# Linear attention and MLP on one core: splitting the second pair's columns from loaded columns, not storing and reloading the split, and one load moved in SyncE's queue

## The chip, the cores and the metric

The kernel runs on one core of a Trainium2 chip. The metric is the device time of one execution in microseconds, median of three runs. A core has five engines with queues of their own: TensorE (PE in the profile; its weight loads are PEld), VectorE (DVE), ScalarE (ACT), GpSimd (POOL) and SyncE (SP). In this kernel nearly all transfers are issued from SP's queue, in the order of the program; the bias additions come from POOL's.

## The reference, cut to what matters

Input x is 2048 rows (S) of 512 columns (D); F is 1376; there are 32 heads of 16 columns.

```python
def _A_ref(x, wqkv, wo):                  # linear attention
    q, k, v = ...x @ wqkv...              # 32 heads
    phi = lambda t: jnp.where(t > 0, t + 1, jnp.exp(t)) + 1e-6
    pq, pk = phi(q), phi(k)
    kv = jnp.einsum("bhsd,bhse->bhde", pk, v)
    z = jnp.einsum("bhsd->bhd", pk)
    num = jnp.einsum("bhqd,bhde->bhqe", pq, kv)
    den = jnp.einsum("bhqd,bhd->bhq", pq, z)[..., None] + 1e-6
    return (num / den) @ wo               # heads side by side
def _B_ref(x, w1, b1, w2, b2):            # MLP, squared relu
    r = relu(x @ w1 + b1)
    return (r * r) @ w2 + b2
xn = _layernorm(x)
return x + _A_ref(xn, wqkv, wo) + _B_ref(xn, w1, b1, w2, b2)
```

## The kernel before, in words

**Tiles and blocks.** The 2048 tokens are 16 tiles of 128 rows, and four tiles make a block of 512 tokens (blocks 0 to 3). Each float32 operand of a matmul is used as two parts, a rounded high part (`h`) and the rest (`l`), and a product takes three matmuls (high by high, high by low, low by high; `three`, L127). ACT makes a high part by a copy; DVE makes the low part by a subtraction (`split` L117, `rest_of` L121).

**First half of the program (to about 100 us): keys and the key-value sums.** For each tile in turn SP loads rows of x, the row statistics are taken and the tile is normalised (L248), turned into columns (`transposed`, L312) and split into `xs..h` and `xs..l` (tiles of `xsb`, two pairs: `xsb[0]` = xs0, `xsb[1]` = xs1; blocks 0 and 2 use xs1, blocks 1 and 3 use xs0). Matmuls project the keys (`pk`, L369) and sum keys times tokens (`kx`, L389). Tiles 0 to 3 are turned by PE. From tile 4 on the turning goes by way of HBM: `regroup` (L277) stores the normalised tile (`via`, L281), then four loads bring it back regrouped (`xg`, issued by `move`, L289), and DVE transposes 32 by 32 blocks (`turn`, L293). Columns of tiles 0 to 7 (blocks 0 and 1) are stored unsplit in HBM as well (`xTd`, L336). Those of blocks 2 and 3 stay on chip (`xT2`, `xT3`). The row tiles x0/x1, x2/x3, x12/x13 and x14/x15 share two buffers in turn (`two`, L91): the load of tiles 14 and 15 takes the buffer of tiles 2 and 3. It stands behind `normalise(*single)`, which normalises tile 4 and issues its store, in the program and so in SP's queue (L656, L657).

**Stored parts.** In this half, at tiles 4 and 7, the split columns of blocks 0 and 1 are stored to HBM too, high and low part each as one transfer of 1 MB (`xsd`, L807 to L811), since their buffers are needed again for blocks 2 and 3.

**Second half: two phases `n`.** Phase 0 (to about 252 us) computes the outputs of blocks 3 and 2 (`t1`, `t2`), phase 1 those of blocks 1 and 0. In each phase queries and the MLP's first layer are formed for the pair of blocks by seven-product block multiplications (`product`, L484). Their operands are the split columns `x1`, `x2` (xs0, xs1), sums of column halves (`T`, made from unsplit columns by `sums_of`, L751) and split weight chunks (`aop`, made by `operands_first`, L771, in the buffers of the unsplit columns xT2 and xT3). The remainder of w1 that fills no chunk of 128 is multiplied on its own by `plain_1` (L478), from a split chunk `z` (`w1z`). The second layer and the attention output accumulate in four PSUM banks (`acc`) and are added to the residual rows (`res`, L1054) and stored.

**End of phase 0, where most of the change lies (L1248 to L1341).** PE sums the second layer of block 2 over the hidden tiles in the order of `waiting`, then attention (`add_attention`), then the last two hidden tiles (`last_two`: hidden tile 0 and the remainder, number 10). Their parts are made by `wait_for` (L1225): ACT squares and copies, DVE subtracts. In the steps `e` of the loop the next phase is prepared: the unsplit columns `f1`, `f2` of blocks 1 and 0 come back from `xTd` into xT3 and xT2 (L1254), the four stored parts are reloaded into xs0 and xs1 (L1300 to L1302, one for each of `e` = 1 to 4), the remainder of w1 is loaded at `e` = 4 (`small_chunk`, L785; DMAs of L184) and split at `e` = 7, and two chunks of wqkv are loaded at `e` = 5 (L714).

**What sets the order.** The order on every engine and queue is written out by hand (`manual_schedule`, L76): an engine takes its instructions as the program emits them. The lists `AT` and `AE` and the tuple at L1303 place small steps.

Of the kernel before, what the change touches and what calls it, by code (L numbers as in the profile page):

```python
# [18 lines left out]
def kernel(  # L19
# [71 lines left out]
    def two(name):  # L91
        return keep.tile([P, 2, 512], F32, name=name, tag=next_tag("x"))
# [7 lines left out]
    def f32(ap):  # L100
        return ap.bitcast(F32)
# [7 lines left out]
    def copy(eng, o, i, bias=0.0):  # L109
        if eng == "act":  # L110
            nc.scalar.activation(o, i, AF.Copy, bias=bias)  # L111
        elif bias:
            ENG[eng].tensor_scalar(o, i, bias, None, op0=OP.add)
        else:
            ENG[eng].tensor_copy(o, i)

    def split(h, l, src, eh, el):  # L117
        copy(eh, h, src)
        ENG[el].tensor_tensor(out=l, in0=src, in1=f32(h), op=OP.subtract)  # L119

    def rest_of(l, src, h):  # L121
        nc.vector.tensor_tensor(out=l, in0=src, in1=f32(h), op=OP.subtract)  # L122
# [21 lines left out]
        pair(f"pair_{k}")  # L144
    dram = ctx.enter_context(tc.tile_pool(name="dram", bufs=1, space=bass.MemoryType.DRAM))
    xTd = [dram.tile([P, NJ, BT], F32, name=f"xTd{b}") for b in range(NB // 2)]
    xsd = [[dram.tile([P, NJ, BT], F32, name=f"xsd{b}{u}") for u in "hl"] for b in range(NB // 2)]
    w2s, wos = {}, {}
    ident = keep.tile([P, P], F32, name="ident", tag="ident")
    heads = work.tile([P, P], F32, name="heads", tag="heads")  # L150
# [6 lines left out]
    def load_x(i, t):  # L157
        n = t.shape[1]
        nc.sync.dma_start(t, xf[i * P:(i + n) * P, :].rearrange("(i p) d -> p i d", i=n))
        for k in range(n):  # L160
            xr[i + k] = t[:, k]
# [18 lines left out]
    def raw_1(f):  # L180
        t = w512(f"r1_{f}", "raw", 6)
        tj = t.rearrange("p (j n) -> p j n", j=NJ)
        for a, o, n in units(f):
            nc.sync.dma_start(tj[:, :, a:a + n], w1[:, o:o + n].rearrange("(j p) n -> p j n", j=NJ))  # L184
        return t
# [62 lines left out]
    def normalise(tiles, st, mv, y):  # L248

        n = len(tiles)  # L250
        r, u = (y[:, k, :n] for k in range(2))
        if tiles[-1] >= NPE:

            nc.vector.scalar_tensor_tensor(u, mv[:, :n, 0], -1.0, r, op0=OP.mult, op1=OP.mult)
        later = []

        def last(i, o, src, k):
            nc.scalar.activation(o, src, AF.Identity, bias=u[:, k:k + 1], scale=r[:, k:k + 1])
            if i in groups:
                regroup(i)  # L260

        for k, i in enumerate(tiles):
            o, src = xp[i], xr[i]
            if i >= NDVE:

                o, src = o.rearrange("p g (j c) -> p g j c", j=NJ), gjc(src)
            if i < NPE:
                nc.vector.tensor_scalar(o, src, mv[:, k, 0:1], r[:, k:k + 1], op0=OP.subtract, op1=OP.mult)
                if i in groups:
                    regroup(i)  # L270
            else:
                later.append(lambda a=(i, o, src, k): last(*a))
        return later
# [25 lines left out]
    def cols(i):  # L299

        return xsb[(i // TB + 1) % 2]
# [77 lines left out]
    def phi_k(i, ps, mid=lambda: None, late=lambda: None):  # L379
        kp[i] = w512(f"k{i}", "p", 6)  # L380
        phi(ps, kp[i], mid, late)
# [265 lines left out]
    single = group(4)  # L647
    soon = group(5)
    normalise(*fourth)
    phi_k(0, pks[0])  # L650
    measure(single)
    tokens(0)
# [1 line left out]
    parts(0)  # L654
    phi_k(1, pks[1])
    normalise(*single)  # L656
    load_x(14, two("x14"))  # L657
    parts(1)
    tokens(1, "dve")
    measure(soon)  # L660
# [57 lines left out]
    def load_1(kind, n):  # L718
        load = raw_1 if kind == "w" else raw_q
        return [load(2 * n + k).rearrange("p (c n) -> p c n", c=2) for k in range(2)]  # L720
# [50 lines left out]
    def operands_first(n, w):  # L771

        o = {}

        def first():
            aop.update({k: keep.tile([P, 2, 2, 512], F32R, name=f"aop{n}_{k}", tag=f"xT{NB // 2 + k}") for k in range(2)})
            chunk_split(0, 0, w[0])

        def sums():
            o[0], o[1] = chunk_sums(0, w)  # L780

        return [first, sums, lambda: chunk_split(0, 1, o[0]), lambda: last_split(0, w[1][:, 1]),
                lambda: chunk_split(1, 0, o[1])]

    def small_chunk(z):  # L785
        t = raw_1(NF - 1)
        return lambda: split(z[:, 0], z[:, 1], t, "act", "dve")

    extra, counts = [], [[0, 0, 0, 0, 0, 1, 1, 0, 0, 1, 2, 2, 0, 1, 4, 1, 2]]

# [10 lines left out]
    for i in range(2, NT):  # L801
        if i == 13:
            nc.sync.dma_start(b1s[:, :NF - 1], b1[:(NF - 1) * P].rearrange("(f p) -> p f", p=P))
            for a, o, n in units(NF - 1):
                nc.sync.dma_start(b1s[a:a + n, NF - 1:], b1[o:o + n, None])
        move()
        if i in (4, 7):  # L807

            b = i // 7
            for u in range(2):  # L810
                nc.sync.dma_start(xsd[b][u], f32(cols(b * TB)[u]))  # L811
        if i == 9:
            load_o()
        if i > 10:
            fetch()
        ps = pks[i] if i < 3 else bank(f"pk{i}")
        if i > 2:
            project(i, ps, wk, HL)
        high = low = keep_t = lambda: None
        if i < NDVE:  # L820
            high, low, keep_t = transposed(i + 1)
        later = normalise(*soon) if i == 3 else []

        soon_turned = transposed(i + 2) if 11 <= i and i + 2 < NT else ()

        def mid():
            high()
            more(i)

        def late():  # L830
            low()
            more(i)

        if i == 12:
            rawz = raw_1(NF - 1)
            T.update({n: tokens_sum(n, f"B{n - 1}") for n in (1, 2)})
        if i == 12:
            w = load_1("q", 0)
        if i == 13:
            todo_1 = operands_first(0, w)  # L840
            extra.append(todo_1.pop(1))
        if i == 14:
            z = pair("w1z0")
            extra.append(lambda: split(z[:, 0], z[:, 1], rawz, "act", "dve"))
            o34 = halves(four("Tf", "r0"))
            extra.extend(sums_of(xT[NB - 1], xT[NB - 2], *o34))
            lows = [extra.pop() for k in range(2)]
            extra += [todo_1[0], lows[1], todo_1[1], lows[0], *todo_1[2:]]
        phi_k(i, ps, mid, late)
        more(i)  # L850
        run(*soon_turned)
        if i != 3:
            later = normalise(*soon) if soon else []
        parts(i)
        keep_t()
        if i == 2:
            tokens(2)
        if i + 1 < NT:
            tokens(i + 1)
        run(*later)  # L860
        if NDVE < i + 2 < 13:
            run(*transposed(i + 2))
        pieces(int(i > 11))
        if i == 2:
            ahead[3] = statistics(6, 7)
        if i + 2 in (4, 6, 8, 10):
            ahead[i + 2] = group(i + 6, i + 7)
        if i < 10:
            measure(ahead[(i + 2) // 2 * 2], i % 2)
        soon = ahead.get(i + 1, ())  # L870
        if soon:
            roots(*soon)
        kx(i - 1)
        more(i)
# [66 lines left out]
    for n in range(2):  # L941
# [343 lines left out]
        for e, f in enumerate(waiting[:-2]):  # L1285
            mlp_2(acc, f, s.pop(f))
            if e + 3 < NF - 2:
                wait_for(waiting[e + 3])
            if e:
                do(w2next, 2)  # L1290
                if e + 8 < NF:
                    g = waiting[e + 8]
                    w2next.extend(piece_2(g, place(g)))
            if e == 2:
                load_res(t2)
            if e == 4:
                bias = add_bias()
            if e in ((5, 6) if n else (7, 8)):
                do(bias)
            if n == 0 and 1 <= e < 5:  # L1300
                k, u = divmod(e - 1, 2)
                nc.sync.dma_start(f32((x1, x2)[k][u]), xsd[(t1, t2)[k] - 2][u])  # L1302
            do(prepare, (1, 0, 0, 1, 0, 2, 2, 3, 1, 3, 1)[e])  # L1303
            if n == 0:
                if e == 4:
                    z = pair("w1z1")
                    zs = small_chunk(z)
                if e == 5:
                    w = load_1("q", 0)
                if e == 7:  # L1310
                    zs()
            step(AE[e])
            if e and 0 < len(parts_2) and len(steps[t2]) <= 5 * (len(parts_2) - 1):
                do(parts_2)
# [2 lines left out]
        do(parts_2, NJ)  # L1317
        for k in range(TB):
            add_attention(acc, t2 * TB + k, n == 1 and k == last)
            if k < 2:  # L1320
                wait_for(last_two[1 - k])
            if n == 0:
                if k == 0:
                    prepare = operands_first(1, w)
                if k in (0, 2):
                    do(prepare, 2 if k == 0 else 3)
# [43 lines left out]
```

## Time and profile before

| | |
|---|---|
| median of three runs | 410.08 us (409.76 to 411.25) |
| profiled execution | 410.41 us |
| its span, first to last instruction | 408.7 us |
| PE / DVE / ACT busy | 403.8 / 304.7 / 262.2 us |
| bytes moved by DMA | 56.87 MB |
| granted PE clock | 0.999 |

A row of the chain of work that ended last gives start, length and what ran or was waited for. "SPq" and "DVEq" are a queue's own time for an issue, "DMA a<-b" a transfer that was waited for. A row of the timeline gives start and length, the engine, the line, the operation, out<-in, shapes and a count; in brackets the idle time ahead of it and what ended it. For an SP row the length is the time of the issue, not of the transfer. A row of groups ends with the count, the busy time and the mean in ns, then the idle time ahead and its cause. A row of stretches gives the stretch, its length, and busy time and count for each engine, then PE's clock, the mean busy share of the DMA engines and GB/s. A row of waits gives total, times and longest.

### The profile page before, as it was taken

The page shows a single profiled execution, that of the slowest core. Times are in us where ns is not written, and L with a number is a line of the kernel's source. Part 1 is how long each engine was busy: PE and PEld are TensorE (multiplying, and loading weights), DVE is VectorE, ACT ScalarE, POOL GpSimd, SP SyncE. Part 2 cuts the span into 40 slices and gives each one's busy share as a digit, 9 for nine tenths or more (in the row PEclk, how much of TensorE's full clock was granted, in tenths as well). Part 3 has the DMA queues.
Part 4 walks back from the last instruction along what each step waited for, and adds up shares of the span by engine and source line. Part 5 has one row for each costly group of instructions (what it writes and reads, how often), then busy time and mean ns, then how long its engine had stood idle before and what let it go on. Part 6 is the DMA issues. An engine that isn't in the chain of part 4 may idle for free.

```text
span 408.7 us, 5630 instructions
## 1 busy us (share of the span) xinstructions
PE 403.8 (99%) x1943; PEld 331.7 (81%) x1943; DVE 304.7 (75%) x556; ACT 262.2 (64%) x459; POOL 48.5 (12%) x81
## 2 busy tenths in 40 slices
PE   8999999999999999999999999999999999999996
PEld 7878888888788888888878887888888888878885
DVE  6886667487898989988349956567989586449833
ACT  4656777556888788886818641677587857837520
POOL 6343333220000000030000300000000200001200
PEclk9999999999999999999999999999999999999999
DMA  6969576810432231381557983321121881024612
GB/s 213 332 210 329 204 309 206 254 31 0 119 91 79 77 103 28 109 204 22 215 204 271 326 194 106 113 53 51 51 79 36 229 189 36 2 103 154 105 26 103
DMA packets 47182, 56.87 MB, mean 139 GB/s; under 512 B 8305, under 2 KB 30577, under 8 KB 45874
## 3 DMA queue, kind: packets, MB, share of 16 engines
q1 hardware_dynamic: 44850, 52.32, 39.3%
q0 software_dynamic: 2304, 4.20, 6.3%
q8 instruction: 15, 0.25, 0.2%
q14 instruction: 13, 0.11, 0.1%
HBM read 41.69 MB, written 13.63 MB: 135 GB/s over the span
## 4 chain that ended last, share of the span: by engine, by line
PE 85%; DMA 6%; DVE 5%; issue 1%; SPq 1%; ACT 1%; POOL 1%; DVEq 0%; ACTq 0%
PE b L488 33%; PE acc L130 29%; PE pk L369 9%; PE kx L389 9%; DMA r<-in_B_w_dram 4%; PE acc L499 2%; PE pz L130 1%; DVE s L119 1%; SPq L289 1%; PE b L130 1%; PE pz0b L130 1%; DMA x<-in_A_x_dram 1%; DMA via<-xp 1%; DMA xg4s<-via 1%; PE pt L308 0%
## 5 line engine op out<-in xcount | busy, mean ns | idle before, releaser
L130 PE MATMUL acc<-w2r,s 128*128 128x512 f32 x477 | 113.1, 390 | 0.4 <-DVE s L119 0.4
L130 PEld LDWEIGHTS acc<-w2r,s 128*128 128x128 f32 x477 | 89.4, 188 | 20.1 <-DVE s L119 0.8
L488 PE MATMUL b<-T,aop 128*128 128x512 f32 x336 | 83.4, 389 | 0.0
L488 PEld LDWEIGHTS b<-T,aop 128*128 128x128 f32 x336 | 63.0, 188 | 13.9 <-ACT t L111 0.8
L1046 POOL DMA_DIRECT2D res<-in_B_b_dram x16 | 14.4, 1091 | 277.2 <-DVE dt L430 87.4
L389 PE MATMUL kx<-pk,tok 128*128 128x512 f32 x192 | 46.3, 390 | 0.0
L389 PEld LDWEIGHTS kx<-pk,tok 128*128 128x128 f32 x192 | 35.9, 188 | 7.6
L488 PE MATMUL b<-xs0h,aop 128*128 128x512 f32 x112 | 36.9, 390 | 0.0
L130 PE MATMUL acc<-mh,aTsr 128*128 128x512 f32 x112 | 35.6, 389 | 0.0
L1054 DVE TENSOR_TENSOR res<-acc,res 128x512 f32<-128x512 f32 x16 | 11.0, 692 | 21.5 <-PE acc L130 19.2
L488 PEld LDWEIGHTS b<-xs0h,aop 128*128 128x128 f32 x112 | 21.0, 188 | 4.4
L130 PEld LDWEIGHTS acc<-mh,aTsr 128*128 128x128 f32 x112 | 21.0, 188 | 4.4
L119 POOL TENSOR_TENSOR tok<-xp,tok 128x512 fp32r<-128x512 f32 x15 | 19.8, 1322 | 38.9 <-ACT tok L111 38.9
L122 DVE TENSOR_TENSOR w2r<-r,w2r 128x512 fp32r<-128x512 f32 (+2 forms) x35 | 23.8, 681 | 0.5 <-ACT w2r L111 0.4
L111 ACT ACTIVATE aop<-S 128x512 fp32r<-128x512 f32 x28 | 17.5, 624 | 9.8 <-DVE S L728 9.8
L119 DVE TENSOR_TENSOR aop<-S,aop 128x512 fp32r<-128x512 f32 x28 | 19.3, 688 | 4.8 <-ACT aop L111 4.4
L119 DVE TENSOR_TENSOR s<-c,s 128x512 fp32r<-128x512 f32 x20 | 13.5, 689 | 11.4 <-ACT s L111 11.3
L488 PE MATMUL b<-xs0l,aop 128*128 128x512 f32 x56 | 21.8, 389 | 0.0
L130 PE MATMUL acc<-ml,aTsr 128*128 128x512 f32 x56 | 21.8, 389 | 0.0
L111 ACT ACTIVATE w2r<-r 128x512 fp32r<-128x512 f32 x32 | 19.6, 620 | 3.0 <-DMA out_dram<-res 2.0
L111 ACT ACTIVATE T<-Tf 128x512 fp32r<-128x512 f32 x16 | 9.5, 624 | 16.1 <-DVE Tf L671 16.0
L488 PE MATMUL b<-xs1h,aop 128*128 128x512 f32 x56 | 19.5, 389 | 0.0
(190 smaller groups left out, 742.9 us busy)
## 6 DMA issues: line engine op xcount, KB each, us to landing
r<-in_B_w_dram SPq DMA_DIRECT2D x49, 256.0 KB, 3.0
res<-in_A_x_dram SPq DMA_DIRECT2D x8, 512.0 KB, 4.2
res<-in_B_b_dram POOLq DMA_DIRECT2D x16, 256.0 KB, 5.8
out_dram<-res SPq DMA_DIRECT2D x15, 256.0 KB, 2.1
via<-xp SPq DMA_DIRECT2D x5, 512.0 KB, 3.2
xg<-via SPq DMA_DIRECT2D x20, 128.0 KB, 2.8
xTd<-t SPq DMA_DIRECT2D x8, 256.0 KB, 3.2
x<-in_A_x_dram SPq DMA_DIRECT2D x4, 512.0 KB, 6.4
```

The source lines that it names most:

```text
L111: nc.scalar.activation(o, i, AF.Copy, bias=bias)
L119: ENG[el].tensor_tensor(out=l, in0=src, in1=f32(h), op=OP.subtract)
L122: nc.vector.tensor_tensor(out=l, in0=src, in1=f32(h), op=OP.subtract)
L130: nc.tensor.matmul(ps, lhsT=a[u], rhs=b[v], start=first and n == 0, stop=last and n == 2)
L289: nc.sync.dma_start(*moves.pop(0))
L369: nc.tensor.matmul(ps, lhsT=cols(i)[u][:, j, slot(i)], rhs=w[v][:, j, :], start=first and n == 0, stop=last and n == len(steps) - 1)
L389: nc.tensor.matmul(kxp[c], lhsT=tok[i][:, u, c * P:(c + 1) * P], rhs=pk[i][:, v], start=i == 0 and (u, v) == first, stop=i == NT - 1 and ( ...
L488: nc.tensor.matmul(ps, lhsT=a[u][:, j * P:(j + 1) * P], rhs=b[v][:, j, :], start=first and j == 0 and n == 0, stop=last and j == 1 and n == 2,
L499: nc.tensor.matmul(ps, lhsT=s[u][:, k * P:(k + 1) * P], rhs=w2s[NF - 1][u][:, a:z], start=first and u == 0, stop=stop and u == 1)
L1046: nc.gpsimd.dma_start(r[:, i], b2[None, :].partition_broadcast(P), accum_op=OP.add)
L1054: nc.vector.tensor_tensor(out=r[:, a:z], in0=ps, in1=r[:, a:z], op=OP.add)
```

## The change

The parts of blocks 0 and 1 are no longer stored and reloaded: the HBM tiles `xsd`, four stores and four loads go (1 MB each). In their place, at the end of phase 0, ACT makes the high parts of xs1 (`columns_high(x2, f2)`, at `e` = 6) and of xs0 (at `e` = 7, behind the split of `z`) from the loaded unsplit columns, each in two instructions of 1024 columns, and DVE makes the low parts (`columns_low`), also in two each: those of xs1 ahead of the parts of the last two hidden tiles, those of xs0 behind them. The parts of the last two hidden tiles are now both formed ahead of the weight operands of phase 1 in phase 0; before, the operands' first step stood between them. The load of w1's remainder is issued at `e` = 3 and that of the two wqkv chunks at `e` = 4, each one step earlier. The load of tiles 14 and 15 stands in front of tile 4's store. The order on PE is the same; DVE and ACT have the four wide instructions each, and SP has eight DMAs fewer.

```diff
-    xsd = [[dram.tile([P, NJ, BT], F32, name=f"xsd{b}{u}") for u in "hl"] for b in range(NB // 2)]
...
     normalise(*fourth)
+    load_x(14, two("x14"))
     phi_k(0, pks[0])
...
     normalise(*single)
-    load_x(14, two("x14"))
     parts(1)
...
-    def small_chunk(z):
-        t = raw_1(NF - 1)
-        return lambda: split(z[:, 0], z[:, 1], t, "act", "dve")
+    def columns_high(x, t):
+
+        for a in range(0, NJ, 2):
+            copy("act", x[0][:, a:a + 2], t[:, a:a + 2])
+
+    def columns_low(x, t):
+
+        for a in range(0, NJ, 2):
+            rest_of(x[1][:, a:a + 2], t[:, a:a + 2], x[0][:, a:a + 2])
...
-        if i in (4, 7):
-
-            b = i // 7
-            for u in range(2):
-                nc.sync.dma_start(xsd[b][u], f32(cols(b * TB)[u]))
...
-            if n == 0 and 1 <= e < 5:
-                k, u = divmod(e - 1, 2)
-                nc.sync.dma_start(f32((x1, x2)[k][u]), xsd[(t1, t2)[k] - 2][u])
             do(prepare, (1, 0, 0, 1, 0, 2, 2, 3, 1, 3, 1)[e])
             if n == 0:
+                if e == 3:
+                    rawz = raw_1(NF - 1)
                 if e == 4:
                     z = pair("w1z1")
-                    zs = small_chunk(z)
-                if e == 5:
                     w = load_1("q", 0)
+                if e == 6:
+                    columns_high(x2, f2)
                 if e == 7:
-                    zs()
+                    split(z[:, 0], z[:, 1], rawz, "act", "dve")
+                    columns_high(x1, f1)
...
             add_attention(acc, t2 * TB + k, n == 1 and k == last)
-            if k < 2:
+            if n == 1 and k < 2:
                 wait_for(last_two[1 - k])
             if n == 0:
                 if k == 0:
+                    columns_low(x2, f2)
+                    for f in reversed(last_two):
+                        wait_for(f)
+                    columns_low(x1, f1)
                     prepare = operands_first(1, w)
```

## The prediction

> **What bounds the kernel now.** I read the page first, then the chain that ended last in order of time, then TensorE's (PE's) timeline where that chain leaves PE, then the queues of ScalarE (ACT), VectorE (DVE) and SyncE (SP) there.
>
> ```profile
> span 408.7 us, 5630 instructions
> ...
> PE 403.8 (99%) x1943; PEld 331.7 (81%) x1943; DVE 304.7 (75%) x556; ACT 262.2 (64%) x459; POOL 48.5 (12%) x81
> ```
>
> PE is busy almost without a break. What the change can win is therefore not transfer time but the few places where PE stops. Stretches of the span show where:
>
> ```profile
> 28.00:240.00 212.00, 212.00 (x1087) 173.98 (x1088) 166.51 (x298) 148.25 (x258) 27.41 (x39) 1.00 0.52 162
> 240.00:250.00 10.00, 9.59 (x43) 7.60 (x42) 7.76 (x15) 4.40 (x8) 0.00 (x0) 1.00 0.31 83
> 250.00:400.00 150.00, 150.00 (x667) 123.67 (x666) 104.45 (x191) 93.44 (x162) 7.08 (x8) 1.00 0.34 91
> ```
>
> The columns after the length are busy times of PE, PEld, DVE, ACT, POOL, then PE's clock, the DMA share and GB/s. From 28 to 400 us PE is idle only inside 240 to 250. The chain has two detours that this change touches: one at 18 to 28 us and one that ends at 248 us.
>
> ```profile
> 18.49 2.36 DMA via<-xp
> 21.30 2.32 SPq L289
> ...
> 197.46 10.88 PE acc L130 x48
> ...
> 224.46 16.91 DMA r<-in_B_w_dram
> ...
> 248.21 0.50 PE acc L130
> ...
> 252.60 2.72 PE pz L130 x12
> 255.32 4.08 PE b L488 x18
> ```
>
> 48 matmuls in 10.88 us is 0.2267 us for each 512-column matmul: PE's pace. The gaps follow from PE's timeline at the two places:
>
> ```profile
> 24.94 2.88 PE L389 MATMUL kx<-pk,tok 128*128 128x512 f32 x12
> 27.89 0.50 PE L369 MATMUL pk<-wkh,xs0h 128*128 128x512 f32 x1
> 28.23 0.39 PE L369 MATMUL pk<-wkl,xs0h 128*128 128x512 f32 x1
> ...
> 247.18 0.62 PE L130 MATMUL acc<-w2r,s 128*128 128x512 f32 x2
> 248.21 0.50 PE L130 MATMUL acc<-w2r,s 128*128 128x512 f32 x1 [0.41 <-DVE s L119]
> 248.54 0.63 PE L499 MATMUL acc<-w2r,s 128*128 128x512 f32 x2
> ```
>
> Middle gap: the next matmul was due at 247.18 + 2 x 0.227 = 247.63 and began at 248.21, 0.58 late; its successor came 0.33 after it, not 0.23, another 0.10. Together 0.68 us. Early gap: due at 24.94 + 12 x 0.2267 = 27.66, began at 27.89, successor 0.34 later: 0.23 + 0.11 = 0.34 us.
>
> **The change, part by part.**
>
> *Stores removed (four of 1 MB, first half).* They leave SP's queue and the DMA engines between 34 and 70 us. PE has 212.00 busy of 212.00 us there, so I price them at nothing; the cover is PE's own queue of matmuls. Without that cover the price would be the time by which the stores hold up the regrouping (via) behind them, at most the longest wait of this row:
>
> ```profile
> SPq L289 <- DMA via<-xp: 14.6, 6, 4.4
> ```
>
> *Reloads removed (four of 1 MB, 214 to 223 us).* In SP's queue they stand right ahead of the w1 remainder (three DMAs, L184), the two wqkv chunks (L714) and a small copy:
>
> ```profile
> 222.76 0.43 SPq L1302 DMA_DIRECT2D xs1l<-xsd0l  x1
> 223.29 10.97 SPq L184 DMA_DIRECT2D r<-in_B_w_dram  x3
> ...
> 223.30:241.40 18.10, 18.10 (x81) 14.98 (x81) 13.90 (x24) 7.45 (x13) 3.54 (x4) 1.00 1.07 305
> ```
>
> The last row is the stretch itself: DMA share 1.07, 305 GB/s. Three reloads (3 MB) and 1 MB of residuals are in front; the remainder's three issues hold SP for 10.97 us, and its last part lands 16.91 us after its issue, at 241.4. Without the reloads it is issued at about 222 (it is also asked for one step earlier), and 1.3 MB, the residuals with it, take 4.3 us at 305 GB/s, 8.5 at half of that: it lands before 231. The first time ACT can use it is 237.6 (below). The chunks move forward with it.
>
> *Work added.* ACT makes four 1024-column copies and DVE four 1024-column subtractions, forms that the trace lacks. From the nearest rows:
>
> ```profile
> L111 ACT ACTIVATE aop<-rq 128x512 fp32r<-128x512 f32 x1 | 0.6, 634 | 0.8 <-DVE Tf L671 0.8
> L111 ACT ACTIVATE aop<-rq 128x256 fp32r<-128x256 f32 x1 | 0.4, 399 | 0.0
> ```
>
> ACT: 235 ns per 256 columns, so 634 + 2 x 235 = 1.10 us each, 4.4 us in all. DVE (rows 245.39 and 246.00 below): 0.69 and 0.42, so 0.69 + 2 x 0.27 = 1.23 us each, 4.9 us in all. Bounds: the cost of two 512-column instructions (1.27 and 1.38) above, one (0.63 and 0.69) below. Whether this is hidden shows in the two queues:
>
> ```profile
> 229.78 1.90 ACT L111 ACTIVATE w2r<-r 128x512 fp32r<-128x512 f32 x3
> 236.25 1.36 ACT L111 ACTIVATE T<-Tf 128x512 fp32r<-128x512 f32 x2 [4.57 <-DVE Tf L671]
> 241.48 0.63 ACT L111 ACTIVATE w1z<-r 128x512 fp32r<-128x512 f32 x1 [3.87 <-DMA r<-in_B_w_dram]
> ...
> 236.25 1.42 DVE L671 TENSOR_TENSOR Tf<-xT,Tf 128x512 f32<-128x512 f32 x2
> 242.14 0.69 DVE L119 TENSOR_TENSOR w1z<-r,w1z 128x512 fp32r<-128x512 f32 x1 [4.47 <-ACT w1z L111]
> ...
> 245.39 0.69 DVE L119 TENSOR_TENSOR aop<-rq,aop 128x512 fp32r<-128x512 f32 x1
> 246.00 0.42 DVE L728 TENSOR_TENSOR S<-rq 128x256 f32<-128x256 f32 x1
> ...
> 249.01 0.69 DVE L119 TENSOR_TENSOR aop<-S,aop 128x512 fp32r<-128x512 f32 x1
> ```
>
> ACT's first two copies (pair xs1) stand between the second and third w2r and fall into the idle 4.57 us. After T (ends 237.6) come w1z (to 238.3, no longer waiting 3.87), the two xs0 copies (to 240.5), then the last hidden tiles' heads: 0.6 each, with one square, done at 242.4. DVE goes on at 237.7 with w1z's rest (from 238.3), Tf and two T rests (to 240.9), two xs1 rests (to 243.4), the 64-row rest (to 244.1), and s, which PE waits for: done at 244.8. PE asks for it at 247.63, so 2.8 us are to spare, and the whole middle gap goes: -0.68.
>
> What is queued behind on DVE: two xs0 rests (to 247.3), then the next pair's weight operands, which ended at 249.7 and now end at about 251.1 (the same instructions: two of 0.69 and four of 0.42 or less among them). By the chain's last two rows, less 0.68, PE begins on xs0 at 251.9 and on the operands at 254.6, so neither is late. The first bank that the second phase reuses is freed by a residual add (0.69) right behind the operands, at 251.8, 2.8 us ahead of its use; the stores and w1 loads that SP has behind those adds shift by some tenths. Behind that nothing is known to be late: PE was busy 150.00 of 150.00 us from 250 to 400, so the gain stays to the end.
>
> *The load of tiles 14 and 15* (512 KB) moves ahead of tile 4's store, on SP.
>
> ```profile
> 14.26 0.55 DVE L268 TENSOR_SCALAR xp<-x,mv,y 128x512 f32<-128x512 f32 x1 [0.20 <-POOL xp L346]
> ...
> 18.89 0.43 SPq L159 DMA_DIRECT2D x<-in_A_x_dram  x1
> 19.67 0.52 SPq L336 DMA_DIRECT2D xTd<-t  x1
> ...
> 17.50:18.00 0.50, 0.50 (x4) 0.41 (x3) 0.50 (x2) 0.00 (x0) 0.38 (x1) 1.00 1.07 418
> 18.00:18.50 0.50, 0.50 (x4) 0.42 (x3) 0.47 (x1) 0.49 (x1) 0.00 (x0) 1.00 0.47 176
> ...
> 25.68 0.63 DVE L245 TENSOR_SCALAR y<-mv 128x2 f32<-128x2 f32 x1
> 26.46 0.71 DVE L293 STREAM_TRANSPOSE t<-xg4s 128x512 f32<-128x512 f32 x1 [0.15 <-DMA xg4s<-via]
> ```
>
> Its buffer is free when tile 3 is normalised (14.81), so it is issued at about 15, 3.5 us before the store's 18.49 in the chain, and holds up no issue. Its data is another matter: the engines ran full until about 18.2 (share 1.07, then 0.47), so 512 KB more at some 400 GB/s (the row has 418) keeps them full for another 1.3, until 19.5. The store, which took 2.36 us to land, lands 0 to 1.3 later. Against that, the regrouping loads behind it now meet only one transposed-tile store (issued at 19.67) in the queue, not that and the 512 KB, so the issue of 2.32 us should shrink towards the 0.43 of the other issues: 0 to 1.9 us earlier. I take the middles, 0.65 later and 0.95 earlier: DVE finds its data before it is free. It is busy with statistics until 26.31 and began the transpose at 26.46, so the gain ends at 0.15. I take 0.1; the ends are -0.15 and +1.3.
>
> The Trainium skill, page "DMA: Bandwidth & Descriptors", section "Queues, rings and completion order", speaks against this part: each DMA engine takes its descriptors in ring order, so the store waits behind the whole 512 KB. By that rule the early step costs 1.3, if the issue stays long, and the sum is +0.6 where mine is -0.8; that is the first rival.
>
> **Sum.** -0.68 - 0.1 = -0.8 us. The profiled execution took 410.41 us around its span of 408.7: 409.6. The median of the three runs shown, 410.08, is 0.3 lower than that execution: 409.3. I say 409.4.
>
> **Rivals.**
>
> *Store queued behind the load (other side).* The store lands 1.3 later and the second regrouping issue still takes 2.32 us. Then the transpose begins at 27.8, and PE's early gap grows by 1.3: -0.68 + 1.3 = +0.6, some 410.7 to 411.0. It decides once the early loss is over 0.68. For: the engines are full to 18.2. Against: the long issue came right behind this very load, which now is 3.9 us earlier. Chance 0.15.
>
> *The column work comes late.* ACT's or DVE's added 4 to 5 us push s past 247.63. It needs 2.8 us more than I worked out; even the upper bounds add only 4 x 0.17 and 4 x 0.15, 1.3 us. If it happened by a further 3 us, the middle gap would be 3 us and the time about 412.6. Chance 0.05.
>
> *The middle gap stays.* Something else, such as the small copies' landing, ends that wait: the change does not do what it seems to, and the time is 410.0. For: DVE's work on s was released by ACT, not by a DMA. Against: ACT itself waited 3.87 for the w1 remainder. Chance 0.08.
>
> *Less traffic helps beyond the gaps.* 8 MB of transfers go. Yet PE is busy 18.10 of 18.10 us, with 81 matmuls, where the DMA share is 1.07 (4.5 a microsecond; from 250 to 400, at 0.34, 667 in 150, 4.4), and both gaps together hold 1.0 us. Over 2 us of gain, 408.0, would need something that no row shows. Chance 0.04.
>
> **How the numbers follow.** The forecast case has the remaining 0.68: 409.4, by itself 408.9 to 410.0 (the three runs lay from 409.76 to 411.25, so a median moves by some tenths). The 8-in-10 range takes in the gap that stays and the queued store: 408.6 to 411.1. About 2 us, 0.5%, is what a measurement here can tell from no change; the forecast, the staying gap and the queued store all lie within it. Faster by more: 0.05. Slower by more, from late columns, a queued store with more behind it, and the runs' spread: 0.09. Within: 0.86.
>
> **What would show it.** Middle: PE's timeline near 247 without a wait for s, w1z on ACT right behind T near 237.7, the remainder's three issues within 2 us. Early: the first matmul on xs0h at about 27.8, no issue of 2.3 us at L288. ACT's copies near 1.1 and DVE's rests near 1.2 us. I would be wrong if the store's landing moves to 22 or later, or if the w1 remainder still lands after 238.

## The result and the profile after

The changed kernel takes 409.66 us in the median (409.43 to 410.38), the kernel before 410.48 (409.76 to 411.29) on the same chip: a ratio of 0.9981, 95% interval 0.9975 to 0.9988. It is 0.8 us faster, which is less than the 0.5% bound that the prediction set.

The execution that the profiler recorded took 410.38 us, however, the longest of the 22 shown, against 410.41 before. Its page and two of its stretches (28 to 240 and 240 to 250 us), columns as in the prediction:

```profile
span 408.7 us, 5625 instructions
...
PE 402.7 (99%) x1943; PEld 331.0 (81%) x1943; DVE 308.9 (76%) x560; ACT 265.8 (65%) x463; POOL 48.4 (12%) x81
...
DMA packets 46030, 48.48 MB, mean 119 GB/s; under 512 B 8177, under 2 KB 30449, under 8 KB 45746
```

```profile
28.00:240.00 212.00, 211.38 (x1084) 173.51 (x1085) 168.28 (x301) 152.41 (x264) 27.35 (x39) 1.00 0.44 126
240.00:250.00 10.00, 10.00 (x46) 8.28 (x45) 9.88 (x15) 4.26 (x8) 0.00 (x0) 1.00 0.06 15
```

PE's idle time has changed places: 240 to 250 is full (10.00, before 9.59), but the stretch that was full, 28 to 240, lacks 0.6. DVE and ACT are busy 4.2 and 3.6 us longer, and 8.4 MB less is moved. The chain of work that ended last, in order of time, shows the place:

```profile
18.66 5.09 DMA via<-xp
23.82 0.34 SPq L288
...
25.15 1.92 DMA xg4s<-via
27.19 0.72 DVE t L292
27.93 0.64 ACT xs0h L323
28.61 3.02 PE pk L368 x12
...
209.69 39.01 PE acc L130 x171
252.55 2.72 PE pz L130 x12
```

Tile 4's store took 5.09 us to land where it took 2.36, and the chain behind it reaches PE. At 248 us, where the chain left PE for a DMA and for DVE before, it now stays on PE (39.01 us, 171 matmuls). The timelines of PE, SP, ACT and DVE at both places:

```profile
25.09 2.88 PE L388 MATMUL kx<-pk,tok 128*128 128x512 f32 x12
28.61 0.50 PE L368 MATMUL pk<-wkh,xs0h 128*128 128x512 f32 x1 [0.64 <-ACT xs0h L323]
28.95 0.40 PE L368 MATMUL pk<-wkl,xs0h 128*128 128x512 f32 x1
247.85 0.85 PE L130 MATMUL acc<-w2r,s 128*128 128x512 f32 x3
...
23.82 1.76 SPq L288 DMA_DIRECT2D xg4s<-via  x4
222.47 1.56 SPq L183 DMA_DIRECT2D r<-in_B_w_dram  x3
...
238.19 0.61 ACT L111 ACTIVATE w1z<-r 128x512 fp32r<-128x512 f32 x1
238.71 1.99 ACT L111 ACTIVATE xs0h<-xT 128x1024 fp32r<-128x1024 f32 x2
...
241.25 2.36 DVE L122 TENSOR_TENSOR xs1l<-xT,xs1h 128x1024 fp32r<-128x1024 f32 x2
244.35 0.69 DVE L119 TENSOR_TENSOR s<-r2c,s 128x512 fp32r<-128x512 f32 x1
250.36 0.68 DVE L119 TENSOR_TENSOR aop<-S,aop 128x512 fp32r<-128x512 f32 x1
```

*Early gap.* The matmul on xs0h was due at 25.09 + 12 x 0.2267 = 27.81 and began at 28.61, 0.80 late, with 0.11 more at its successor: 0.91 us, where it was 0.34. *Middle gap.* Three matmuls on `w2r,s` run without a break from 247.85, so the 0.68 is gone; s is done at 245.04 and is asked for by the third, at 247.85 + 2 x 0.227 = 248.30. So in this pair of executions 0.68 was won and 0.57 lost, and PE came to the kx row 0.15 later (25.09, before 24.94): together 0.04 us longer, where the execution was in fact 0.03 shorter. Between this pair, then, nothing was gained, while the medians differ by 0.8. The question is therefore what a typical execution of each kernel looks like.

### The profile page after: what moved, and what is told of

Same layout as the page of the kernel before. It is cut to its first block, busy times and chain, and to the rows that moved or that the text cites. A ratio compares the mean times of both kernels' runs of the same rounds, so it can differ in the third digit from the quotient of the medians.

```text
span 408.7 us, 5625 instructions
## 1 busy us (share of the span) xinstructions
PE 402.7 (99%) x1943; PEld 331.0 (81%) x1943; DVE 308.9 (76%) x560; ACT 265.8 (65%) x463; POOL 48.4 (12%) x81
## 4 chain that ended last, share of the span: by engine, by line
PE 94%; DMA 2%; DVE 1%; ACT 1%; POOL 1%; SPq 0%; issue 0%; DVEq 0%
PE acc L130 37%; PE b L487 33%; PE pk L368 9%; PE kx L388 9%; PE acc L498 2%; PE pz L130 1%; DMA via<-xp 1%; DMA x<-in_A_x_dram 1%; PE b L130 1%; PE pz0b L130 1%; DMA xg4s<-via 0%; PE pt L307 0%; PE acc L505 0%; DVE st L233 0%; PE pkv L908 0%; POOL tok L119 0%
## 5 line engine op out<-in xcount | busy, mean ns | idle before, releaser
L487 PE MATMUL b<-xs1h,aop 128*128 128x512 f32 x56 | 19.5, 389 | 0.0
```

The costliest lines, as they stand in the source:

```text
L487: nc.tensor.matmul(ps, lhsT=a[u][:, j * P:(j + 1) * P], rhs=b[v][:, j, :], start=first and j == 0 and n == 0, stop=last and j == 1 and n == 2,
```

## Experiments

**Two more profiles of the changed kernel, without an edit.**

> The changed kernel as it is, for a second profile and a time on the same chip as the three runs beside it. Theory A (the whole gain is the middle gap of 0.68 us, the moved load is worth about nothing in a typical run): 0.998 of before, and an early gap on PE that differs from profile to profile, between 0.2 and 0.9 us, with the time following it. Theory B (the moved load costs some 0.6 us in every run, as the profile of after has it, and the middle is worth 1.4): an early gap near 0.9 us again, tile 4's store landing after 5 us again.

Measured: 409.58 us (409.45 to 410.29), kernel before on that chip 410.81 (409.58 to 412.61), ratio 0.9973 [0.9960, 0.9985]. PE and SP in the profile, an execution of 409.59 us:

```profile
25.18 2.88 PE L388 MATMUL kx<-pk,tok 128*128 128x512 f32 x12
27.91 0.42 PE L368 MATMUL pk<-wkh,xs0h 128*128 128x512 f32 x1
...
18.68 0.34 SPq L280 DMA_DIRECT2D via<-xp  x1
22.47 1.76 SPq L288 DMA_DIRECT2D xg4s<-via  x4
```

Due 25.18 + 2.72 = 27.90, began 27.91: no early gap, and no middle gap either. The regrouping loads (issued when the store has landed) begin 3.79 behind the store's issue, between before's 2.43 (18.49 to 20.92) and the first profile's 5.16.

> The changed kernel again, as the reference on this chip for the three runs beside it. Median 409.6; PE's early gap anywhere from 0 to 0.9 us in its profile.

Measured: 409.80 us (409.46 to 410.46), before on that chip 410.89 (410.11 to 413.24), ratio 0.9976 [0.9967, 0.9986]; its profile (409.70) has neither gap. Over all comparisons 32 of 44 executions of the changed kernel lie at or below 409.8 us and none above 410.5; of the kernel before 7 of 124 do, and 86 lie above 410.5. The lowest are 409.43 and 409.58. So the change hardly lowers the floor: executions near it become the rule instead of the exception. What follows reads this as waits that are there in some executions and not in others. The kernel before has only one profile, so how often it has which wait is not shown.

**Which part does it? The column work alone, and the load alone.** The first puts the load back behind tile 4's store, the second makes only that move in the kernel before.

```diff
     normalise(*fourth)
-    load_x(14, two("x14"))
...
     normalise(*single)
+    load_x(14, two("x14"))
```

> The changed kernel with the load of tiles 14 and 15 back behind tile 4's store. Theory A: -0.7 us against before (0.9983), the same as the whole change within 0.2 us; PE's early gap 0.34 as before, no middle gap. Theory B: -1.4 us (0.9966), faster than the whole change by some 0.6 us.

```diff
     normalise(*fourth)
+    load_x(14, two("x14"))
...
     normalise(*single)
-    load_x(14, two("x14"))
```

> The kernel before with only the load of tiles 14 and 15 in front of tile 4's store. Theory A: within 0.2 us of before (0.9995 to 1.0005), middle gap of about 0.7 us still there. Theory B: +0.6 us (1.0015). By the prediction's own step: -0.1 us.

Measured, on the chip of the first repeat: columns only 410.14 us (409.59 to 410.40), 0.9982 [0.9968, 0.9997]; load only 409.96 us (409.48 to 410.98), 0.9983 [0.9970, 0.9997]. The parts give 0.67 and 0.85 in the median, both together 1.23; with intervals of 0.3% their order is not settled. The load counts on top of the columns too: 11 of 12 executions of the whole change are at or below 409.72, and 2 of 12 with the columns only. Both theories missed on the load: A had it within 0.2 us of before, B had it slower, and it was 0.85 faster. Columns only has no early gap either, where theory A kept 0.34. The profile of the load alone (409.53 us) was the surprise. ACT, DVE and PE at 247 us:

```profile
240.62 0.63 ACT L111 ACTIVATE w1z<-r 128x512 fp32r<-128x512 f32 x1 [3.17 <-DMA r<-in_B_w_dram]
246.61 0.69 DVE L119 TENSOR_TENSOR s<-r2c,s 128x512 fp32r<-128x512 f32 x1
247.02 0.85 PE L130 MATMUL acc<-w2r,s 128*128 128x512 f32 x3
```

Reloads and order are those of before, the remainder is late as before (ACT waits 3.17 for it), and still there is no middle gap: s is done at 247.30, the third matmul asks at 247.47. The step stands near its due time: 0.58 late in one execution, 0.17 in time in the other. The same three issues of the remainder behind the same reloads held SP for 10.97 us in the one and 10.00 in the other.

**Which half of the column work takes the middle gap?** The change both moves s ahead of the operands and frees the remainder from the reloads. Each alone, in the kernel before:

```diff
-            if k < 2:
+            if n == 1 and k < 2:
                 wait_for(last_two[1 - k])
             if n == 0:
                 if k == 0:
+                    for f in reversed(last_two):
+                        wait_for(f)
                     prepare = operands_first(1, w)
```

> The kernel before, stores and reloads kept, with only one step changed: the parts of the last two hidden tiles are both formed ahead of the weight operands of the second phase. Theory A1 (the middle gap exists because s stands behind the operands on DVE, 2.1 us of other work): s is ready at about 246.1 though the remainder still lands at 241.4, the gap goes, -0.7 us (0.9983). Theory A2 (it exists because the remainder lands late behind the reloads, and only the traffic's going removes it): the gap stays at 0.4 us or more, time within 0.3 us of before.

```diff
+            if n == 0 and e == 2:
+                zs_raw = raw_1(NF - 1)
             if n == 0 and 1 <= e < 5:
...
-                    zs = small_chunk(z)
+                    zs = lambda: split(z[:, 0], z[:, 1], zs_raw, "act", "dve")
```

> The kernel before, stores and reloads kept and the order on DVE and ACT as it was, with only the load of w1's remainder moved ahead of the last three reloads on SP. Theory A2: the remainder lands before 231, w1z on ACT follows T at about 237.6, s is ready near 243.6, the gap goes, -0.7 us. Theory A1: the lateness of the remainder is not what holds s, the gap stays. Both runs without a gap: either half of the change was enough.

Measured, before on that chip 411.07 us (409.65 to 412.98): order 410.20 (409.43 to 412.05), 0.9976 [0.9958, 0.9993]; remainder 410.34 (409.65 to 411.13), 0.9978 [0.9964, 0.9992]. ACT, DVE and PE with the order alone, then with the remainder alone:

```profile
241.29 0.63 ACT L111 ACTIVATE w1z<-r 128x512 fp32r<-128x512 f32 x1 [3.47 <-DMA r<-in_B_w_dram]
245.21 0.69 DVE L119 TENSOR_TENSOR s<-r2c,s 128x512 fp32r<-128x512 f32 x1
247.39 0.85 PE L130 MATMUL acc<-w2r,s 128*128 128x512 f32 x3
```

```profile
238.26 0.61 ACT L111 ACTIVATE w1z<-r 128x512 fp32r<-128x512 f32 x1
246.32 0.69 DVE L119 TENSOR_TENSOR s<-r2c,s 128x512 fp32r<-128x512 f32 x1
247.93 0.85 PE L130 MATMUL acc<-w2r,s 128*128 128x512 f32 x3
```

Either is enough, to judge by the margins: that a gap is missing says little, since the load-only profile lacks it too. With the order alone the remainder is as late as ever, yet s is done at 245.90, 1.9 ahead of its matmul; with the remainder alone s is done at 247.01, 1.4 ahead; with neither it was 0.58 late and 0.17 in time. For this gap the 8 MB need not go.

**How much room has the added work?** The rests of xs1 are formed three times over, the same values again: 4.5 us more on DVE ahead of s (6.90 where the changed kernel has 2.36).

```diff
-                    columns_low(x2, f2)
+                    for _ in range(3):
+                        columns_low(x2, f2)
```

> The changed kernel with the low parts of xs1 computed three times over (the same values; 4.7 us more on DVE ahead of s). By the prediction's margin (s ready 2.8 us ahead of PE): a wait on PE for s of 4.7 - 2.8 = 1.9 us, time +1.9 us against the whole change. If the margin is larger than worked out, because DVE had slack elsewhere, the wait is shorter; if s is not what PE needs first there, no wait shows.

Measured: 411.04 us (410.91 to 411.84), 1.0002 [0.9986, 1.0019]; that is 1.2 to 1.5 above the changed kernel's three medians, none of them taken beside it, where 1.9 was expected. DVE and PE:

```profile
241.29 6.90 DVE L122 TENSOR_TENSOR xs1l<-xT,xs1h 128x1024 fp32r<-128x1024 f32 x6
248.94 0.69 DVE L119 TENSOR_TENSOR s<-r2c,s 128x512 fp32r<-128x512 f32 x1
...
247.89 0.62 PE L130 MATMUL acc<-w2r,s 128*128 128x512 f32 x2
249.69 0.50 PE L130 MATMUL acc<-w2r,s 128*128 128x512 f32 x1 [1.17 <-DVE s L119]
```

The gap that the prediction's "late columns" rival described appears: the matmul was due at 247.89 + 2 x 0.227 = 248.34, so 1.35 late, 1.46 with its successor. That is about the added 4.5 less the spare 3.26 (245.04 to 248.30 in the first profile of the changed kernel), not less 2.8: that execution had PE 0.67 later at this place than the prediction took it, which widened the margin. This profile has an early gap too, 1.04 us.

**Are the stores free?** All four stores put back into the changed kernel, where nothing reads them (`xsd` and the four lines at `i in (4, 7)` as in the kernel before); then only block 0's two (`i == 4`), then only block 1's two (`i == 7`).

```diff
         move()
+        if i in (4, 7):
+            b = i // 7
+            for u in range(2):
+                nc.sync.dma_start(xsd[b][u], f32(cols(b * TB)[u]))
```

> The changed kernel with the four stores of 1 MB put back, read by nothing. By the prediction (stores priced at nothing, PE's queue covers them): the same as the whole change within 0.2 us, no PE gap from 28 to 400 us, the waits for via on SP longer again. Rival (the stores cost something in the first half): up to 0.8 us more, the whole gain of the change.

Measured: 410.51 us (410.00 to 411.56), 0.9987 [0.9970, 1.0003]. The changed kernel was not timed beside it; its three comparisons gave 0.9981, 0.9973 and 0.9976, and the intervals overlap. None of the 12 executions is below 410.0; 34 of 44 of the changed kernel's are at or below it. But the stores alone do not bar the floor: the kernels with only the load or only the order changed keep all four, and their lowest are 409.48 and 409.43. The profile has a gap that neither original kernel's profile had. The chain, and ACT and PE there:

```profile
68.60 3.91 DMA via<-xp
...
73.85 4.55 DMA xg<-via
78.60 0.72 DVE xT L293
79.34 0.63 ACT xs0h L324
```

```profile
79.34 0.63 ACT L324 ACTIVATE xs0h<-xT 128x512 fp32r<-128x512 f32 x1 [3.49 <-DVE xT L293]
78.92 1.07 PE L369 MATMUL pk<-wkh,xs0l 128*128 128x512 f32 x4
80.69 3.00 PE L389 MATMUL kx<-pk,tok 128*128 128x512 f32 x12 [0.71 <-ACT pk L111]
```

The regrouping of tiles 14 and 15, the last, comes late by way of HBM, DVE's transpose and ACT's copy wait for it, the key copy `pk` is queued behind that copy on ACT, and PE stands: due at 78.92 + 4 x 0.227 = 79.83, began 80.69.

> The changed kernel with only the first pair of stores put back (34 us, parts of block 0). Theory S1 (the gap of 0.9 us at 79.7 us with all four stores comes from the first pair: it holds tile 9's store for 6 us, and DVE and ACT carry that lateness on to the last regrouping at 68 us): a gap near 80 us in the profile, +0.5 to +0.9 us against the changed kernel. Theory S2 (it comes from the second pair at 54 us): no gap there, time the same within 0.2 us.

> The changed kernel with only the second pair of stores put back (54 us, parts of block 1). Theory S1: no gap near 80 us, time the same as the changed kernel within 0.2 us. Theory S2: the gap is there, +0.5 to +0.9 us. By the prediction's price of nothing for the stores, neither this run nor the one with the first pair differs from the changed kernel.

Measured: block 0's stores 410.14 us (409.75 to 410.80), 0.9983 [0.9973, 0.9994]; block 1's 410.28 (409.92 to 410.96), 0.9984 [0.9972, 0.9997]; the changed kernel on that chip 409.80, 0.9976 [0.9967, 0.9986]. So 0.34 and 0.48 us more in the median, which these intervals do not tell from nothing. Neither profile has a gap at 80 us, so neither theory, S1 or S2, came out. What each pair does to the queue does show: it holds up the regrouping right behind it. Here are the store of tiles 12 and 13 and its regrouping loads, first without block 1's stores (the changed kernel, third profile), then with all four:

```profile
58.27 0.34 SPq L280 DMA_DIRECT2D via<-xp  x1
60.91 1.73 SPq L288 DMA_DIRECT2D xg<-via  x4
```

```profile
58.56 0.32 SPq L281 DMA_DIRECT2D via<-xp  x1
62.33 1.74 SPq L289 DMA_DIRECT2D xg<-via  x4
```

From the first row to the second it is 2.62 to 2.64 us in the eight profiles without block 1's stores and 3.04 to 3.96 in the six with them. For tiles 8 and 9, behind block 0's stores, it is 5.9 to 6.3 us with these and 2.7 without (3.30 where the load of tiles 14 and 15 stands there). SP's waits for `via` come to 9.5 to 13.3 us in all in the seven profiles without stores, 15.0 and 13.8 with one pair, and 14.6 to 17.9 in the five with all four. DVE's wait for tiles 14 and 15 at 70 to 79 us is 3.2 to 3.8 in the nine profiles without all four, and 2.9, 4.1, 5.1, 5.5 and 6.1 with them; at 5.5 and 6.1 (the remainder-early kernel and this one) PE has a gap at 80 us. How the lateness gets from there to tiles 14 and 15, whose store is issued some 14 us after the last of block 1's, is less plain: their loads start 3.45 to 3.93 us behind that store in four of the six kernels with block 1's stores, but 2.65 and 2.72 in the other two, against 2.66 to 3.05 without. The stores do not always hold PE up. They widen a wait, and in two of five profiles with all four PE stops behind it.

**Where should the load stand?** Two further places: behind the regrouping loads of tiles 6 and 7, at `i == 4` (34 us), and between tile 4's regrouping loads and tile 5's store (23.5 us), the same with `i == 2`.

```diff
     normalise(*fourth)
-    load_x(14, two("x14"))
...
         move()
+        if i == 4:
+            load_x(14, two("x14"))
```

> The changed kernel with the load of tiles 14 and 15 behind the regrouping loads of tile 7 (some 34 us), away from tile 4's store on both sides. If the load disturbs the store or the regrouping loads at either place, both go: the store lands in 2.4 us or less, no issue of 2.3 us, PE's early gap falls to the 0.2 us that DVE's statistics leave, and the time is 0.1 to 0.2 us below the whole change (theory A) or 0.6 to 0.7 us (theory B). A loss is possible if the load in its new place holds up the regrouping of tiles 8 and 9; PE has no gap there now.

> The changed kernel with the load of tiles 14 and 15 between the regrouping loads of tile 4 and tile 5's store (some 22.5 us), where the two earlier profiles show DMA engines nearly idle (23 to 24.5 us). If the load delays tile 4's store when in front of it and the first regrouping loads when right behind it, it now does neither: store landed within 2.4 us, last regrouping issue of tile 4 before 23 us, PE's early gap below 0.1 us, and the runs close to the fastest seen, 409.4 to 409.7, narrower than the changed kernel's. If the median is the same as the changed kernel's within 0.1 us, the place in front of the store costs nothing in a typical run. A loss would show as a wait at tile 5's transpose (PE at about 33.5 us).

Measured: late 409.94 us (409.57 to 410.77), 0.9981 [0.9968, 0.9995], 0.36 above the changed kernel on that chip; between 410.96 (410.54 to 412.48), 1.0005 [0.9992, 1.0018], 1.16 above it on its chip. For both, no loss was expected first. Both profiles have the detour again, one or two tiles later. The chain of the late one, then of the one between:

```profile
33.73 4.19 DMA xg<-via
37.94 0.72 DVE t L292
...
39.37 1.66 PE pk L368 x6
```

```profile
24.03 4.46 DMA via<-xp
...
29.81 2.00 DMA xg4s<-via
...
35.37 3.05 DMA xg<-via
```

Late, the load is issued at 34.20, behind the fourth regrouping load of tiles 6 and 7, and PE stops for 0.72 at 39.4. Between, tile 5's store is issued half a microsecond behind the load and lands after 4.46; PE stops at 33.8 and 39.9 for 0.58 and 0.55. The place in front of tile 4's store, 3.6 us ahead of it, has the lowest median of the four tried, and no kernel here beat the changed one; only the loss of the place between is clear of the intervals.

**All profiles side by side.** Two rows of PE's timeline split each execution: the start of the kx group ahead of tile 4, and of the last group of the program. The gaps are those behind the first row, worked out as above.

| kernel | execution, us | kx group | last group | between | gaps seen |
|---|---|---|---|---|---|
| before | 410.41 | 24.94 | 405.05 | 380.11 | 0.34 + 0.68 |
| changed, first | 410.38 | 25.09 | 405.03 | 379.94 | 0.91 |
| changed, second | 409.59 | 25.18 | 404.26 | 379.08 | none |
| changed, third | 409.70 | 25.28 | 404.38 | 379.10 | none |
| columns only | 409.90 | 25.40 | 404.55 | 379.15 | none |
| load only | 409.53 | 25.09 | 404.20 | 379.11 | none |
| order only | 409.87 | 25.41 | 404.55 | 379.14 | none |
| remainder early | 410.45 | 25.48 | 405.08 | 379.60 | about 0.4, at 80 us |
| stores kept | 411.02 | 25.09 | 405.39 | 380.30 | 0.94, at 80 us |
| block 0's stores | 410.45 | 25.64 | 404.74 | 379.10 | none |
| block 1's stores | 410.22 | 25.46 | 404.51 | 379.05 | none |
| low rests three times | 411.84 | 24.98 | 406.51 | 381.53 | 1.04 + 1.46 |
| load late | 410.31 | 25.04 | 404.97 | 379.93 | 0.72 |
| load between | 410.88 | 25.15 | 405.53 | 380.38 | 0.58 + 0.55 |

Without a gap the stretch takes 379.1 us, whatever the kernel and its traffic, and the gaps account for the rest to within 0.26. The first 25 us vary by 0.70 between executions and follow no part of the change.

## Why the prediction was right, and where it was not

The time (409.4 predicted, 409.66 measured), the sum (-0.8, medians -0.82) and the forecast that the change would be smaller than 0.5% came out. Not every term did, and that the sum fits to 0.02 is partly luck: the medians differ by 1.23 and 1.09 in the two other comparisons, the start of 410.08 was the median of three executions where 22 gave 410.48, and the terms below missed in both directions.

*Middle gap, -0.68: right in mechanism and nearly to the tenth, for an execution that has the gap.* w1z stands right behind T, the remainder's three issues take 1.56 us, s is done at 245.04 (244.8 predicted), the operands at 251.04 (251.1). The runs with the order or the remainder alone, and with the low rests three times, bear the path out. The forms that the trace lacked, by groups of the changed kernel:

```profile
L122 DVE TENSOR_TENSOR xs1l<-xT,xs1h 128x1024 fp32r<-128x1024 f32 x2 | 2.4, 1222 | 0.0
L111 ACT ACTIVATE xs0h<-xT 128x1024 fp32r<-128x1024 f32 x2 | 2.0, 1045 | 0.0
```

1.22 and 1.05 us, predicted 1.23 and 1.10 from the slope between 256 and 512 columns. (The Trainium skill, page "VectorE: DVE Perf Modes", section "The TRN2 errata", gives a formula for a float32 `tensor_tensor` add; an estimate by it for 1024 columns is 1.224 us, and the trace agrees, with 1.222 for this subtraction.) What failed is taking one execution's 0.68 as the kernel's: the load-only profile has the old order and the old reloads, and no gap.

*Stores, "I price them at nothing": the cover that this rests on failed in two profiles.* It was read from one execution, 212.00 of 212.00 us. With all four stores the regroupings behind them are late in every profile, and in two of five the lateness reaches PE, 0.94 and about 0.4 us, by the very path that the prediction named as the price without cover; in none of the nine others is there a gap at 80 us. What this costs in the median is not settled: 0.9987 with all four put back against 0.9973 to 0.9981 without, with overlapping intervals. PE was full, but a few microseconds of slack in the queue behind it were not looked at.

*Moved load, "0.65 later, 0.95 earlier", -0.1: both halves were under-sized, and their signs were right; the whole is not explained.* The start of the regrouping loads came 3.4 to 5.2 us behind the store's issue in all eight profiles with the load in front, and 2.1 to 2.9 in the six without: 0.9 to 2.7 later than before's 2.43, not 0 to 1.3. (In the first profile the engines were full until 20.0 us, share 1.06, where the prediction has 19.5, and the store landed only at 23.75.) The four issues took 1.76 (one 1.98) in place of 2.75 to 3.66 where the load is behind the store: 1.0 to 1.9 earlier. From the store's issue to the end of the last regrouping issue it is 5.2 to 5.6 in six of the eight, 6.4 and 6.9 in the two with an early gap (1.04 and 0.91), and 5.1, 5.2, 5.5 and 6.1 in the four with the load behind, the last being before's with 0.34. The profiles show no gain on balance; yet the medians on one chip show half a microsecond or more (columns only 410.14, the changed kernel 409.58; before 410.81, load only 409.96), where the prediction has 0.1. Where that lies, none of the profiles says, and it stays open.

*The mark "wrong if the store's landing moves to 22 or later"* was met in seven of the eight profiles with the load in front (21.95 in the eighth, stores kept), and the time was right all the same: the mark watched the half that became worse and not the issues behind it, which became better.

*Rivals.* The queued store (0.15) is what the first profile shows, 0.91 us of gap by way of a landing of 5.09, but only 2 of 8 profiles with the load in front have it, and its second half, the long issue of 2.32, is in none: the four issues take 1.75 to 1.98. The Trainium skill's rule of ring order ("DMA: Bandwidth & Descriptors", "Queues, rings and completion order") has its direction borne out by the landings above, 0.9 to 2.7 us later; it says nothing of the slack behind them, into which the delay fits in 6 of the 8. Late columns: not so, until 4.5 us were added. The staying gap: not so. Less traffic beyond the gaps: not so, since the stretch without a gap is 379.1 us with the 8 MB (load only, order only) and without.

## What to carry to other kernels

A wait of half a microsecond in one profile is one draw. Before pricing its removal, work out by how much the step was late or in time, look at a second execution if there is one, and count the transfers that share its queue; here steps within some half a microsecond of their due time were gaps in one execution and none in another. Taking traffic from a kernel whose busiest engine is full then pays, as far as this case shows, not in that engine's busy time but in how seldom such a step is late. And when a load is moved ahead of a store, ask both what the store's landing loses and what the issues behind it gain.

## What the runs showed of the hardware that was not expected

A 256 KB store issued 0.5 to 3.7 us behind a 512 KB load was followed by its dependent loads after 3.4 to 5.2 us, against 2.1 to 2.9 with no load ahead, though at the rate in the profile (418 GB/s) the load would be done in 1.3 (an estimate, 512 KB over that rate). The four regrouping issues took 1.75 to 2.35 us without that load right in front of them and 2.75 to 3.66 with it. Nearly the same instructions brought PE to the same point at 24.94 to 25.64 us in 14 executions, all at a granted clock of 0.999 to 1.000.
